# Linear attention and Mish layers on Trainium2: separate kinds of PSUM banks for a block's two output tiles, and an earlier start for the dense stage's first rows

## The chip, the cores and the metric

The kernel runs on one core of one Trainium2 chip. The metric is device time in microseconds (us) of one execution; the median of several runs is compared. A profiled execution gives the trace that the text quotes: start and end of the instructions on each engine and of the transfers.

## The reference, cut to what matters

`x` has 2048 rows of 640 numbers (float32). Two layers are run, each with the same weights: a Hedgehog linear attention with 32 heads of 20, then a dense part with 1536 hidden units.

```python
def _A_ref(x, wqkv, w_phi, wo):                      # on the layernorm of x
    q, k, v = split_heads(x @ wqkv)                  # 32 heads of 20
    pq, pk = q @ w_phi, k @ w_phi                    # per head, 20 x 20
    phi_q = concatenate([softmax(pq), softmax(-pq)]) # 40 features per head
    phi_k = concatenate([softmax(pk), softmax(-pk)])
    kv, z = phi_k^T v, sum_s phi_k                   # over all 2048 rows
    o = (phi_q kv) / (phi_q z + 1e-6)
    return merge_heads(o) @ wo

def _B_ref(x, w1, b1, w2):                           # on the layernorm of x
    h = x @ w1 + b1                                  # 640 -> 1536
    return (h * tanh(softplus(h))) @ w2              # Mish, 1536 -> 640

x = x + _A_ref(layernorm(x), ...)
x = x + _B_ref(layernorm(x), ...)
x = x + _A_ref(layernorm(x), ...)
x = x + _B_ref(layernorm(x), ...)
```

## The kernel before

**Tiles.** The rows are taken in 8 blocks (`NB`) of 256 rows, each block as 2 tiles (`BT`) of 128. A product in float32 is made of three matmuls: each operand is held as a high part and a low part, and high times high, high times low and low times high are added in PSUM. So a weight is a pair of tiles (`r1h`/`r1l`, `r2h`/`r2l`), and transposed rows are a pair `xth`/`xtl`.

**Stages.** In each layer `attend_first` computes the features of queries and keys, adds up the sums over keys in PSUM, and stores each block's query features, transposed, to a DRAM tensor `e_d[b]`. The query tiles of the last block are finished late, by a generator `rest`, of which each `next(rest)` moves what is pending on by one step; its last steps issue the four stores (line 400) of a query tile. Then `attend_second` runs over the blocks, and `dense` follows, with hidden products (L631), Mish (L644 to L657) and the second product (L673), then a residual add.

**A block of `attend_second`.** The change lies here. For block b there are these pieces:

- `load(b)` (L431 and on) fetches the query features `e_d[b]` into two `big` tiles and an `ol` tile. `fetch` (L358) brings the block's 256 rows of x, 640 KB, into one of two x buffers (`xt`).
- `average(b, t)`: 44 matmuls (L531) give numerators and denominators of tile t in PSUM, in an `mm` tile; VectorE evacuates them (L540, L541, L544) into a row tile `xn`, of which there are four.
- `Transposed(...).all()`: three steps, each with TensorE transposes (L275) into a `one` tile, ScalarE's copy to the high part (L113, `xth`), and VectorE's subtraction for the low part (L281, `xtl`). These have an order of their own on ScalarE (`act`).
- `project_half` (L318): 15 matmuls for one half (320 columns) of the output of one tile, with the weights `o_ws`.
- the residual: VectorE adds the PSUM result to the x rows. For tile 0 both halves lie in one `mm` tile and are added at once, 640 wide (L587), with statistics after it (L248, L250). For tile 1 each half lies in a `one` tile and is added by itself (`add_half`, L552, with its statistics in L553; L600 joins them). GpSimd and VectorE make the layernorm's scale and offset (`norm_scale`, L257 to L260). The rows are stored to `x1_d` (L602), from which the dense part reads them.
- `makes[b]` and `fetches[b + 1]`: the dense part's weights, fetched raw (L138) and split by ScalarE (L113) and GpSimd (L146), one of eight groups per block.

Averages run one block ahead: in block b's turn TensorE makes `average(b + 1, ...)`, products of block b, and the transposes of block b + 1 between the two halves of tile 1.

**PSUM** has eight banks: two `mm` tiles of two banks each, and four `one` tiles of one bank each. A new tile waits until the readers of the tile that had its buffer are done.

**What sets the order.** Inside `attend_second` the instructions of TensorE (PE) and of the DMA queue of SyncE (SP) stand in the order in which the code issues them (`manual_schedule`). VectorE (DVE), ScalarE (ACT) and GpSimd (POOL) are ordered by a planner, which simulates the program in time, except for the chain of `act`. Each engine works through its own instructions in order: one that waits holds up those behind it.

**The passage to `dense`.** After block 6's turn the kernel calls `begin_next`, which fetches the first block of the stored rows `x1_d` into a `big` tile and normalizes its two tiles on ScalarE into two row tiles (`xn`). The object it returns is used in block 7's turn: `nxt.all()` transposes it, ahead of block 7's products, so that `dense` can begin right behind them.

```python
                if b < NB - 1:
                    cur = nxt
                if b == NB - 2:
                    nxt = begin_next()
```

Of the kernel before, what the change touches and what calls it, by code (L numbers as in the profile page):

```python
# [8 lines left out]
F32 = mybir.dt.float32  # L9
F32R = mybir.dt.float32r  # L10
AF = mybir.ActivationFunctionType
ALU = mybir.AluOpType
# [4 lines left out]
P = 128  # L17
# [25 lines left out]
def kernel(  # L43
# [22 lines left out]
    def mm_tile():  # L66
        return psum.tile([P, 2, 512], F32, tag="mm", name="mm", bufs=2)

    def one_tile():
        return psum.tile([P, 512], F32, tag="one", name="one", bufs=4)  # L70
# [173 lines left out]
    def norm_stats(t, xt):  # L244

        bn = work.tile([P, 2, 6], F32, tag="bn", name="bn", bufs=2)
        for c in range(2):
            nc.vector.bn_stats(bn[:, c], xt[:, t, c * HC:(c + 1) * HC])  # L248
        mv = work.tile([P, 2], F32, tag="mv", name="mv", bufs=3)
        nc.vector.bn_aggr(mv, bn)  # L250
        return mv
# [60 lines left out]
    def project_half(ps, xts, t, ws, col, c, ks=range(KD)):  # L312
        sl = slice(t * P, (t + 1) * P)
        cs = slice(col + c * HC, col + (c + 1) * HC)
        for k in ks:
            h, l, wh, wl = xts.hs[k], xts.ls[k], ws[k][0][:, cs], ws[k][1][:, cs]
            for n, (a, r) in enumerate(((h, wh), (h, wl), (l, wh))):
                nc.tensor.matmul(ps[:, :HC], a[:, sl], r, start=(k == 0 and n == 0),  # L318
                                 stop=(k == KD - 1 and n == 2))
# [194 lines left out]
                nc.vector.tensor_copy(kvb[:80, 5, :42], ps[:80, 1, :42])  # L514
        yield

    def attend_second(x_src, x_dst, acc, fetches, makes, begin_next):
        kva, kvz, o_ws, loaded, rest = acc
        rows = {}

        def average(b, t):

            phs = loaded[b]
            po = mm_tile()
            for g in range(G):
                n = 120 if g < 10 else 80
                w = GW if g < 10 else 42
                c, j = divmod(g, 8)
                for q in range(2):
                    s0 = t * P + 64 * q  # L530
                    nc.tensor.matmul(  # L531
                        po[64 * q:64 * q + 64, c, GW * j:GW * j + w], phs[g][:n, s0:s0 + 64],
                        kvb[:n, g // 2, 64 * (g % 2):64 * (g % 2) + w], start=True, stop=True)
            o = row_tile()
            den = work.tile([P, H], F32, tag="r", name="den", bufs=2)
            pv = [po[:, c, :(DH + 1) * n].rearrange("p (h d) -> p h d", d=DH + 1)
                  for c, n in ((0, 24), (1, 8))]
            hh = (slice(0, 24), slice(24, H))
            for c in range(2):
                nc.vector.tensor_scalar_add(den[:, hh[c]], pv[c][:, :, DH], DEN_EPS)  # L540
            nc.vector.reciprocal(den, den)  # L541
            for c in range(2):
                n = hh[c].stop - hh[c].start
                nc.vector.tensor_tensor(o.rearrange("p (h d) -> p h d", d=DH)[:, hh[c]], pv[c][:, :, :DH],  # L544
                                        den[:, hh[c]].unsqueeze(2).to_broadcast([P, n, DH]), op=ALU.mult)
            rows.setdefault(b, []).append(o)
            if t == BT - 1:
                del loaded[b]

        def add_half(ps, xt, t, c, bn):  # L550
            cs = slice(c * HC, (c + 1) * HC)
            nc.vector.tensor_tensor(xt[:, t, cs], ps[:, :HC], xt[:, t, cs], op=ALU.add)  # L552
            nc.vector.bn_stats(bn[:, c], xt[:, t, cs])  # L553

        with tc.manual_schedule(engines={mybir.EngineType.PE, mybir.EngineType.SP}):
            kv = finish_kv(kva, kvz, mask)
            next(rest)
            next(kv)
            loaded[1] = load(1)
            xs = {0: fetch(x_src, 0)}  # L560
            fetches[0]()
            next(rest)
            next(kv)
            next(rest)
            average(0, 0)
            average(0, 1)
            loaded[2] = load(2)
            average(1, 0)
            cur = Transposed(rows.pop(0)).all()
            average(1, 1)  # L570
            loaded[3] = load(3)
            for b in range(NB):
                if b == NB - 1:
                    nxt.all()
                elif b:
                    average(b + 1, 0)
                xt = xs.pop(b)
                py = mm_tile()
                project_half(py[:, 0], cur, 0, o_ws, 0, 0)
                if 0 < b < NB - 1:  # L580
                    average(b + 1, 1)
                    if b + 3 < NB:
                        loaded[b + 3] = load(b + 3)
                if b + 1 < NB:
                    xs[b + 1] = fetch(x_src, b + 1)
                project_half(py[:, 1], cur, 0, o_ws, 0, 1)
                nc.vector.tensor_tensor(xt[:, 0, :].rearrange("p (c d) -> p c d", c=2), py[:, :, :HC],  # L587
                                        xt[:, 0, :].rearrange("p (c d) -> p c d", c=2), op=ALU.add)
                mvs = [norm_stats(0, xt)]
                bn = work.tile([P, 2, 6], F32, tag="bn", name="bn", bufs=2)  # L590
                pa = one_tile()
                project_half(pa, cur, 1, o_ws, 0, 0)
                add_half(pa, xt, 1, 0, bn)
                if b + 1 < NB:
                    nxt = Transposed(rows.pop(b + 1)).all()
                pa = one_tile()
                project_half(pa, cur, 1, o_ws, 0, 1)
                add_half(pa, xt, 1, 1, bn)
                mv = work.tile([P, 2], F32, tag="mv", name="mv", bufs=3)
                nc.vector.bn_aggr(mv, bn)  # L600
                norm_scale(b, mvs + [mv])
                nc.sync.dma_start(row_block(x_dst, b), xt)  # L602
                makes[b]()
                if b + 1 < NB:
                    fetches[b + 1]()
                next(rest, None)
                next(rest, None)
                if b < NB - 1:
                    cur = nxt
                if b == NB - 2:  # L610
                    nxt = begin_next()
            for _ in rest:
                pass
        return nxt


    def dense(x_src, x_dst, w1s, w2s, first, last):
# [117 lines left out]
    with tc.block(schedule_with_timeline_sim=True):  # L735
        src, first = x, None
        for layer in range(LAYERS):
            last = layer == LAYERS - 1
            dst = out if last else x2_d
            acc = attend_first(layer, src, first)  # L740
            if layer == 0:
                nc.sync.dma_start(b1s, b1)
            w1s = []
            w2s = {}

            steps = [("w1", (k,)) for k in range(KD)] + [("w2", fs) for fs in ((0, 1, 2), (3, 4), (5, 6))]

            spares = {("w1", n): [lambda t=t: r1_spare(f"r1{t}")] for n, t in enumerate(("l4", "h4", "l3", "l4"))}
            spares["w1", 4] = [lambda t=t: r2_spare(f"r2{t}") for t in ("h2", "l2", "h3")]
            spares.update({("w2", n): [s] for n, s in enumerate(five_spares(0))})  # L750
            spares["w2", 5] = [lambda: r2_wide(11, F32)[:, 0]]
            spares["w2", 6] = [row_tile]
            raws = {}

            def fetch_step(kind, ns):
                for n in ns:
                    rows = (w1 if kind == "w1" else w2)[n * P:(n + 1) * P, :]
                    raws[n] = fetch_rows(rows, [s() for s in spares[kind, n]])

            def make_step(kind, ns):  # L760
                for n in ns:
                    if kind == "w1":
                        w1s.append(r1_pair(n))
                    else:
                        w2s[n] = w2_pair(n)
                    make_parts((w1s if kind == "w1" else w2s)[n], raws.pop(n), True)

            x1t = []

            def begin_dense():  # L770
                x1t.append(fetch(x1_d, 0, big_tile().rearrange("p (t d) -> p t d", t=BT)))
                return normed(0, x1t[0])

            begun = attend_second(src, x1_d, acc, [lambda s=s: fetch_step(*s) for s in steps],
                                  [lambda s=s: make_step(*s) for s in steps], begin_dense)
            first = dense(x1_d, dst, w1s, w2s, [x1t[0], begun, None], last)
            src = dst

# [37 lines left out]
```

## Time and profile before

| | |
|---|---|
| three runs | 1473.74, 1473.95 (median), 1474.34 us |
| profiled execution | 1471.67 us, of which the span of the trace is 1469.6 us |
| granted TensorE clock, mean | 0.994 of full speed |
| instructions | 27963 |
| data moved | 135.26 MB, mean 92 GB/s |

The page gives busy time and its share of the span by engine. PE stands for TensorE's matmuls, PEld for its weight loads, which overlap them. A line of instructions has the form "line, engine, operation, output<-input"; "L318" is line 318 of the kernel. In the table of waits a row reads "who waits <- for whom: total us, number of times, longest". In the chain of waits a row is a start in us, a duration, and the work that the end of the program hung on at that time. In a table by windows a row has the window, its length, then the busy time and count of PE, PEld, DVE, ACT and POOL, the granted clock, the busy share of the 16 DMA engines and GB/s. In a timeline a row is a start, a duration, the engine, and in brackets the idle time before it and what ended it.

`attend_second` lies at about 270 to 398 us of the span in the first layer and at 990 to 1118 us in the second.

### The profile page before, as it was taken

The page shows a single profiled execution, that of the slowest core. Times are in us where ns is not written, and L with a number is a line of the kernel's source. Part 1 is how long each engine was busy: PE and PEld are TensorE (multiplying, and loading weights), DVE is VectorE, ACT ScalarE, POOL GpSimd, SP SyncE. Part 2 cuts the span into 40 slices and gives each one's busy share as a digit, 9 for nine tenths or more (in the row PEclk, how much of TensorE's full clock was granted, in tenths as well). Part 3 has the DMA queues.
Part 4 walks back from the last instruction along what each step waited for, and adds up shares of the span by engine and source line. Part 5 has one row for each costly group of instructions (what it writes and reads, how often), then busy time and mean ns, then how long its engine had stood idle before and what let it go on. Part 6 is the DMA issues. An engine that isn't in the chain of part 4 may idle for free.

```text
span 1469.6 us, 27963 instructions
## 1 busy us (share of the span) xinstructions
PE 1421.3 (97%) x11748; PEld 1394.3 (95%) x11748; DVE 1053.7 (72%) x1750; ACT 581.2 (40%) x973; POOL 455.1 (31%) x344
## 2 busy tenths in 40 slices
PE   7999999999799999999999999998988999999998
PEld 7999999889799999999999999998978999999998
DVE  4898877667487777777769777867665766666665
ACT  3534334212253444444454344332124444444443
POOL 1454433243242221222235334332443321111111
PEclk9999999999999999999999999999998999999999
DMA  9543334899410000011453342358973001011000
GB/s 297 164 89 57 54 51 71 196 247 249 157 35 19 37 37 10 28 37 37 156 195 66 57 70 54 55 100 203 264 230 118 8 13 37 37 37 37 37 14 24
DMA packets 215023, 135.26 MB, mean 92 GB/s; under 512 B 169977, under 2 KB 190969, under 8 KB 214897
## 3 DMA queue, kind: packets, MB, share of 16 engines
q1 hardware_dynamic: 214897, 133.47, 34.4%
q8 instruction: 92, 1.51, 0.4%
q14 instruction: 34, 0.28, 0.1%
HBM read 84.95 MB, written 48.50 MB: 91 GB/s over the span
## 4 chain that ended last, share of the span: by engine, by line
PE 79%; DVE 10%; ACT 4%; issue 3%; DMA 2%; POOL 1%; SPq 0%; DVEq 0%; POOLq 0%; ACTq 0%
PE mm L318 31%; PE mm L673 17%; PE one L631 17%; PE one L318 6%; PE one L275 3%; PE one L387 3%; PE mm L531 3%; DVE big L646 2%; DVE big L653 1%; DVE big L654 1%; ACT big L644 1%; DVE big L647 1%; DVE big L655 1%; ACT big L648 1%; DMA xt<-in_x 1%
## 5 line engine op out<-in xcount | busy, mean ns | idle before, releaser
L673 PE MATMUL mm<-r2h,ol 128*128 128x320 f32 x1280 | 302.9, 310 | 0.7 <-POOL ol L657 0.5
L657 POOL TENSOR_TENSOR ol<-big,ol 128x512 fp32r<-128x512 f32 (+1 forms) x98 | 127.4, 1300 | 493.5 <-ACT ol L656 393.4
L631 PE MATMUL one<-xtl,r1h 128*128 128x256 f32 x960 | 268.8, 280 | 1.9 <-DVE xtl L281 1.8
L631 PE MATMUL one<-xth,r1h 128*128 128x256 f32 x960 | 270.1, 281 | 0.1
L631 PE MATMUL one<-xth,r1l 128*128 128x256 f32 x960 | 268.3, 279 | 0.0
L673 PEld LDWEIGHTS mm<-r2h,ol 128*128 128x128 f32 x1280 | 219.1, 188 | 1.9 <-POOL ol L657 1.6
L673 PE MATMUL mm<-r2l,ol 128*128 128x320 f32 x640 | 197.9, 309 | 0.0
L318 PE MATMUL mm<-r1h,xth 128*128 128x320 f32 x600 | 189.1, 315 | 0.0
L318 PE MATMUL mm<-r1h,xtl 128*128 128x320 f32 x600 | 186.0, 310 | 0.0
L318 PE MATMUL mm<-r1l,xth 128*128 128x320 f32 x600 | 185.8, 310 | 0.0
L631 PEld LDWEIGHTS one<-xtl,r1h 128*128 128x128 f32 x960 | 180.7, 188 | 2.7 <-DVE xtl L281 2.7
L631 PEld LDWEIGHTS one<-xth,r1h 128*128 128x128 f32 x960 | 180.7, 188 | 0.7 <-ACT xth L113 0.5
L631 PEld LDWEIGHTS one<-xth,r1l 128*128 128x128 f32 x960 | 180.7, 188 | 0.0
L646 DVE TENSOR_SCALAR big<-big 128x512 f32<-128x512 f32 (+1 forms) x98 | 82.1, 837 | 132.7 <-ACT big L644 124.0
L318 PE MATMUL mm<-r2h,xth 128*128 128x320 f32 x460 | 147.2, 320 | 0.0
L318 PE MATMUL mm<-r2l,xth 128*128 128x320 f32 x460 | 142.9, 311 | 0.0
L318 PE MATMUL mm<-r2h,xtl 128*128 128x320 f32 x460 | 142.8, 310 | 0.0
L648 ACT ACTIVATE big<-big,two 128x512 f32<-128x512 f32 (+1 forms) x98 | 70.1, 716 | 164.3 <-DVE big L647 164.2
L113 ACT ACTIVATE xth<-one 128x512 fp32r<-128x512 f32 x144 | 70.3, 522 | 162.8 <-PE one L275 162.4
L656 ACT ACTIVATE ol<-big 128x512 fp32r<-128x512 f32 (+1 forms) x98 | 61.0, 622 | 173.1 <-DVE big L655 172.9
L353 POOL TENSOR_TENSOR r<-r,r 128x1280 f32<-128x1280 f32 x32 | 76.5, 2391 | 161.1 <-DVE r L352 160.9
L673 PEld LDWEIGHTS mm<-r2l,ol 128*128 128x128 f32 x640 | 120.4, 188 | 0.0
(122 smaller groups left out, 3097.1 us busy)
## 6 DMA issues: line engine op xcount, KB each, us to landing
e_d<-r SPq DMA_DIRECT2D x128, 160.0 KB, 4.0
big<-e_d SPq DMA_DIRECT2D x32, 600.0 KB, 8.7
xt<-x_d SPq DMA_DIRECT2D x30, 640.0 KB, 3.9
x_d<-xt SPq DMA_DIRECT2D x23, 640.0 KB, 3.8
xt<-in_x SPq DMA_DIRECT2D x16, 640.0 KB, 4.4
raw<-in_w SPq DMA_DIRECT2D x20, 320.0 KB, 8.3
raw<-in_w SPq DMA_DIRECT2D x8, 768.0 KB, 9.8
out<-xt SPq DMA_DIRECT2D x6, 640.0 KB, 2.9
```

The source lines that it names most:

```text
L113: ins = nc.scalar.activation(*args, **kw)
L275: nc.tensor.transpose(ps[:, c, t * P:(t + 1) * P], self.rows[t][:, (c0 + c) * P:(c0 + c + 1) * P], ident)
L318: nc.tensor.matmul(ps[:, :HC], a[:, sl], r, start=(k == 0 and n == 0), stop=(k == KD - 1 and n == 2))
L353: nc.gpsimd.tensor_tensor(eg, eg, r.unsqueeze(2).to_broadcast([P, 2 * H, DH]), op=ALU.mult)
L387: nc.tensor.matmul(acc[64 * n:64 * n + m, c:c + w], v[:, GW * g:GW * g + m], e[:, 120 * g:120 * g + w], start=(i == 0 and p in (0, 4)), st ...
L531: nc.tensor.matmul(po[64 * q:64 * q + 64, c, GW * j:GW * j + w], phs[g][:n, s0:s0 + 64], kvb[:n, g // 2, 64 * (g % 2):64 * (g % 2) + w], s ...
L631: nc.tensor.matmul(ph[:, j, :], l, r, start=(n == 0), stop=(n == 3 * KD - 1))
L646: nc.vector.tensor_scalar_min(e, e, E_CAP)
L648: nc.scalar.activation(r, n, AF.Ln, bias=two)
L656: nc.scalar.activation(ah[:, js], n, AF.Copy)
L657: nc.gpsimd.tensor_tensor(al[:, js], n, ah[:, js].bitcast(F32), op=ALU.subtract)
L673: nc.tensor.matmul(pys[t][:, c, :HC], l[:, j, sl], r, start=(f == 0 and n == 0), stop=(f == KF - 1 and n == 2))
```

## The change

Four things differ, all in and around `attend_second`.

1. Tile 0's two halves go to two `one` tiles, each with its own 320-wide add and statistics; tile 1's two halves go to the two banks of one `mm` tile, also with an add for each half. A small class `Rows` holds the buffers of a tile's statistics and issues the product and the add.
2. The fetch of the dense part's first rows is a function of its own, called in block 5's turn behind the fetch of block 6's x rows.
3. The normalization of these rows is called in block 6's turn, behind tile 0's second half. It has its own name (`ahead`), and block 7 transposes it as before.
4. In block 0's turn `next(rest)` is called once instead of twice. So the steps of `rest` come one call later from there on, and the stores of a query tile move from block 0's turn to block 1's.

```diff
-        def add_half(ps, xt, t, c, bn):
-            cs = slice(c * HC, (c + 1) * HC)
-            nc.vector.tensor_tensor(xt[:, t, cs], ps[:, :HC], xt[:, t, cs], op=ALU.add)
-            nc.vector.bn_stats(bn[:, c], xt[:, t, cs])
+        class Rows:
+            def __init__(self, b, t):
+                self.t, self.xt, self.ps = t, xs[b], None
+                self.bn = work.tile([P, 2, 6], F32, tag="bn", name="bn", bufs=2)
+
+            def half(self, c, ps):
+                project_half(ps, cur, self.t, o_ws, 0, c)
+                part = self.xt[:, self.t, c * HC:(c + 1) * HC]
+                nc.vector.tensor_tensor(part, ps[:, :HC], part, op=ALU.add)
+                nc.vector.bn_stats(self.bn[:, c], part)
+
+            def mean(self):
+                mv = work.tile([P, 2], F32, tag="mv", name="mv", bufs=3)
+                nc.vector.bn_aggr(mv, self.bn)
+                return mv
...
             for b in range(NB):
                 if b == NB - 1:
-                    nxt.all()
+                    ahead.all()
                 elif b:
                     average(b + 1, 0)
-                xt = xs.pop(b)
-                py = mm_tile()
-                project_half(py[:, 0], cur, 0, o_ws, 0, 0)
+                r0, r1 = Rows(b, 0), Rows(b, 1)
+                r0.half(0, one_tile())
                 if 0 < b < NB - 1:
                     average(b + 1, 1)
                     if b + 3 < NB:
                         loaded[b + 3] = load(b + 3)
                 if b + 1 < NB:
                     xs[b + 1] = fetch(x_src, b + 1)
-                project_half(py[:, 1], cur, 0, o_ws, 0, 1)
-                nc.vector.tensor_tensor(xt[:, 0, :].rearrange("p (c d) -> p c d", c=2), py[:, :, :HC],
-                                        xt[:, 0, :].rearrange("p (c d) -> p c d", c=2), op=ALU.add)
-                mvs = [norm_stats(0, xt)]
-                bn = work.tile([P, 2, 6], F32, tag="bn", name="bn", bufs=2)
-                pa = one_tile()
-                project_half(pa, cur, 1, o_ws, 0, 0)
-                add_half(pa, xt, 1, 0, bn)
+                if b == NB - 3:
+                    fetch_next()
+                r0.half(1, one_tile())
+                mv0 = r0.mean()
+                if b == NB - 2:
+                    ahead = begin_next()
+                py = mm_tile()
+                r1.half(0, py[:, 0])
                 if b + 1 < NB:
                     nxt = Transposed(rows.pop(b + 1)).all()
-                pa = one_tile()
-                project_half(pa, cur, 1, o_ws, 0, 1)
-                add_half(pa, xt, 1, 1, bn)
-                mv = work.tile([P, 2], F32, tag="mv", name="mv", bufs=3)
-                nc.vector.bn_aggr(mv, bn)
-                norm_scale(b, mvs + [mv])
+                r1.half(1, py[:, 1])
+                norm_scale(b, [mv0, r1.mean()])
+                xt = xs.pop(b)
                 nc.sync.dma_start(row_block(x_dst, b), xt)
                 makes[b]()
                 if b + 1 < NB:
                     fetches[b + 1]()
-                next(rest, None)
-                next(rest, None)
+                for _ in range(2 if b else 1):
+                    next(rest, None)
                 if b < NB - 1:
                     cur = nxt
-                if b == NB - 2:
-                    nxt = begin_next()
             for _ in rest:
                 pass
-        return nxt
+        return ahead
...
+            def fetch_dense():
+                x1t.append(fetch(x1_d, 0, big_tile().rearrange("p (t d) -> p t d", t=BT)))
+
             def begin_dense():
-                x1t.append(fetch(x1_d, 0, big_tile().rearrange("p (t d) -> p t d", t=BT)))
                 return normed(0, x1t[0])
```

More of the change, by code (lines that the diff above doesn't have):

```diff
@@ L515, in finish_kv, with attend_second @@
         yield
-    def attend_second(x_src, x_dst, acc, fetches, makes, begin_next):
+    def attend_second(x_src, x_dst, acc, fetches, makes, fetch_next, begin_next):
         kva, kvz, o_ws, loaded, rest = acc
@@ L768 @@
             x1t = []
+            def fetch_dense():
+                x1t.append(fetch(x1_d, 0, big_tile().rearrange("p (t d) -> p t d", t=BT)))
             def begin_dense():
-                x1t.append(fetch(x1_d, 0, big_tile().rearrange("p (t d) -> p t d", t=BT)))
                 return normed(0, x1t[0])
             begun = attend_second(src, x1_d, acc, [lambda s=s: fetch_step(*s) for s in steps],
-                                  [lambda s=s: make_step(*s) for s in steps], begin_dense)
+                                  [lambda s=s: make_step(*s) for s in steps], fetch_dense, begin_dense)
             first = dense(x1_d, dst, w1s, w2s, [x1t[0], begun, None], last)
```

## The prediction

> **What bounds the kernel now.** The page comes first: TensorE is busy for 97% of the span.
>
> ```profile
> PE 1421.3 (97%) x11748; PEld 1394.3 (95%) x11748; DVE 1053.7 (72%) x1750; ACT 581.2 (40%) x973; POOL 455.1 (31%) x344
> ```
>
> So only PE's 48 us without work, and matmuls that run slowly, can be won. The waits of PE, asked for in the two windows that hold `attend_second` (255 to 405 us for the first layer, 970 to 1120 us for the second), say where most of it lies. Columns: total us, times, longest.
>
> ```profile
> PE one L275 <- ACT xn L113: 8.7, 2, 8.4
> PE mm L531 <- DVE xn L544: 3.4, 2, 2.7
> PE one L275 <- DVE xt L552: 0.9, 1, 0.9
> ```
>
> ```profile
> PE one L275 <- ACT xn L113: 8.7, 2, 8.4
> PE one L318 <- DVE xt L552: 2.2, 2, 1.7
> PE one L275 <- DVE xt L552: 1.3, 1, 1.3
> PE mm L531 <- DVE xn L544: 0.7, 1, 0.7
> ```
>
> The long wait is the same in both layers. The chain of waits (start, us, what) shows it around the change of block 6 to block 7:
>
> ```profile
> 364.68 1.41 PE mm L531 x44
> ...
> 374.50 1.09 PE one L275 x10
> 375.60 2.22 PE one L318 x15
> ...
> 380.15 4.97 DMA big<-x_d
> ...
> 385.21 1.74 ACT xn L113 x2
> 386.95 0.04 issue
> 387.00 2.18 PE one L275 x9
> 389.18 4.72 PE mm L318 x30
> ```
>
> ```profile
> 1094.96 2.22 PE one L318 x15
> ...
> 1106.39 2.18 PE one L275 x9
> 1108.57 5.09 PE mm L318 x30
> ```
>
> Block 6's last product ends at 377.82. SP then stores the block, issues weight loads, and only then the fetch of the dense block's rows (4.97 us); ACT normalizes them (1.74), PE transposes them. Block 7's first product starts at 389.18: 11.36 us after block 6's last. In the second layer it is 1097.18 to 1108.57, 11.39 us. Between 364.68 and 377.82, block 6 itself runs without a gap, 13.14 us.
>
> **Part 1, fetch and normalization brought forward.** In the changed program's order of instructions the dense rows' fetch stands on SP in block 5, right behind the x rows of block 6, and the two normalizations stand on ACT ahead of the copies of block 7's transposed rows. The store, the weight loads, the fetch and ACT's first half leave the path. What is late next: there are four row buffers; one holds a weight row and two the averaged rows of block 7, so the second normalization waits until PE has transposed those, and ACT's copies are queued behind it. The DVE and ACT rows of a block give the durations:
>
> ```profile
> 1052.27 1.36 ACT L113 ACTIVATE xth<-one 128x512 fp32r<-128x512 f32 x3 [8.92 <-PE one L275]
> ```
>
> ```profile
> 1052.90 1.62 DVE L281 TENSOR_TENSOR xtl<-one,xth 128x512 fp32r<-128x512 f32 x3
> 1055.13 0.49 DVE L552 TENSOR_TENSOR xt<-one,xt 128x320 f32<-128x320 f32 x1 [0.61 <-PE one L318]
> 1055.65 0.49 DVE L553 BATCH_NORM_STATS2 bn<-xt 128x6 f32<-128x320 f32 x1
> 1056.18 0.21 DVE L600 BATCH_NORM_AGGREGATE mv<-bn 128x2 f32<-128x12 f32 x1
> 1056.55 0.26 DVE L540 TENSOR_SCALAR den<-mm 128x24 f32<-128x24 f32 x2 [0.16 <-PE mm L531]
> 1056.84 0.35 DVE L541 RECIPROCAL den<-den 128x32 f32<-128x32 f32 x1
> 1057.23 0.89 DVE L544 TENSOR_TENSOR xn<-mm,den 128x480 f32<-128x480 f32 x2
> 1059.66 0.23 DVE L260 SCALAR_TENSOR_TENSOR stats<-mv,stats 128x1 f32<-128x1 f32 x2 [1.55 <-POOL stats L258]
> 1065.29 0.82 DVE L587 TENSOR_TENSOR xt<-mm,xt 128x640 f32<-128x640 f32 x1 [3.36 <-DMA xt<-x_d]
> ```
>
> Count from the start of block 7's transposes (374.50 in the first layer). They end at 1.1; the last product of block 6 runs from 1.1 to 3.3. ACT normalizes the second tile from 1.05 to 1.9 (half of 1.74) and copies until 3.3 (1.36). The first two DVE subtractions run 2.5 to 3.9 (two long ones of the 1.62), then block 6's last add (0.49), then the third to 4.8. The dense block's transposes (1.09) begin at 3.3 and end by 4.4, held a little by the buffers that the subtractions free. Block 7's first product follows the third subtraction, at 4.8, that is 1.5 us after block 6's last one instead of 11.4: 9.9 us per layer. The weight copies that ACT has between the two sets of rows are hidden by block 7's products, 2.2 us a half.
>
> Slow matmuls go too: the first 30 took 4.72 and 5.09 us against twice 2.2, so 0.3 + 0.7. Part 1 takes away 2 x 9.9 + 1.0 = **20.8 us**. Bounds: only the transposes' 1.09 left, 21.6; the buffer wait as long again, about 1.5 more in each layer, 17.8.
>
> **Part 2, banks.** The average's second tile now waits for the output tile of the block before, not for the evacuation of the first average. The 3.4 us in the first layer (POOL's work in DVE's queue held that evacuation) and the 0.7 in the second go. In block 0 the first tile's adds stand ahead of a stream transpose, so the 0.9 and 1.3 us of the transposes' waits go. First layer 4.3, second 2.0 at most.
>
> Splitting the 640-wide add costs 2 x 0.49 - 0.82 = 0.16 us of DVE per block, 2.6 us over 16. DVE is not what a block waits for:
>
> ```profile
> 351.60:364.70 13.10, 13.10 (x160) 12.61 (x162) 8.94 (x24) 2.90 (x7) 4.84 (x7) 1.00 0.80 260
> ```
>
> DVE (third busy column) works 8.94 of 13.10 us, so I take nothing. The Trainium skill speaks against such a split ("VectorE: DVE Perf Modes", "The TRN2 errata"): a fixed cost per instruction, so tiles should have at least 512 elements. The trace agrees on the cost, 0.16; by the rule as a price on the path the gain would be 2.6 us less.
>
> **Part 3, what the new order costs.** The first half's add needs the block's x rows, and now stands in DVE's queue *ahead of* the evacuation of the second average, for which the transposes wait. Before, the whole add came behind it. So late rows hurt sooner. And one `next(rest)` moves: the four stores of the last but one query tile go from block 0 to block 1, ahead of that block's loads on SP.
>
> ```profile
> DMA to landing us min/median/max: 4.1/4.7/6.4
> ```
>
> ```profile
> DMA to landing us min/median/max: 3.8/8.8/11.2
> ```
>
> ```profile
> 1028.00:1080.00 52.00, 49.58 (x609) 47.50 (x610) 34.07 (x91) 9.78 (x15) 20.70 (x18) 1.00 1.03 273
> ```
>
> ```profile
> 1017.25 7.36 SPq L400 DMA_DIRECT2D e_d<-r  x4
> ```
>
> ```profile
> 1079.18 0.82 DVE L587 TENSOR_TENSOR xt<-mm,xt 128x640 f32<-128x640 f32 x1 [2.19 <-issue]
> ```
>
> ```profile
> 1081.58 2.47 PE one L318 x15
> ```
>
> The row fetches land after 4.7 us in the first layer, 8.8 in the second, where the DMA engines are full from 1028 to 1080 (share 1.03). There the adds of blocks 4 and 5 (1065.29, 1079.18) already come late; the last half product of block 5 starts 2.4 us after its add began (1081.58). In the new order it must wait for add, statistics, scale terms, evacuation, add, statistics, mean and add: 0.49 + 0.49 + 0.23 + 1.50 + 0.49 + 0.49 + 0.21 + 0.49 = 4.4, with the gaps between them 4.7. If the landings stay where they are, block 5 ends 2.3 us later and the 2.0 of part 2 are swallowed, since the landings, not PE, set the pace. It is no sum over blocks: a PE that waited in block 4 is less early in block 5. If the landings move up with PE (the queue is emptier before block 2, without the four stores), the 2.0 stay. So the second layer lies between -2.0 and +2.3; I take +1.0, nearer the row of a full DMA. In the first layer PE would come to blocks 3 and 4 4.3 us earlier than now, and the rows (4.1 to 6.4) can give some of it back, 0 to 2.7; I take 1.0: -3.3. The extra fetch in block 5 falls behind the full stretch; nothing.
>
> **Sum:** -20.8 - 3.3 + 1.0 = -23.1 us, against the profiled execution's 1471.67 (span 1469.6): 1448.6. The runs' median is 2.28 above that execution, so 1473.95 - 23.1 = **1450.9**.
>
> **Rivals.** *Rows later still.* The four stores (7.36 us of issuing at 1017.25) stand ahead of block 2's loads and push the rows of blocks 3 to 5 back by, say, 4.5 us in both layers, an estimate from half to all of that row. Second layer: 2.3 + 4.5 = 6.8 lost; first: 4.3 gained, some 5.6 lost. -20.8 + 1.3 + 6.8 = -12.7: 1461. For it: the share of 1.03. Against: the same bytes move in the same order but for these four, and the queue had slack just before. Chance 0.13.
>
> *Slower: the loop of two x buffers.* A block's rows can be fetched only when the store of two blocks before has landed. Store (about 10 us in the second layer, taken like a fetch) and fetch (up to 11.2) make 21.2; the new order allows about 2.3 less than the old before PE stops. If this loop, not the DMA's total, sets the landings, each of blocks 1 to 6 loses 2.4 us in both layers: 12 x 2.4 = 29 lost, 20.8 gained, 1482. It decides against the change from 1.8 us a block. For it: waits of 1.7 and 0.5 in the second layer now. Against: the first layer's rows have none, with 4.7. Chance 0.05.
>
> *The fetch doesn't come early.* If the dense rows' buffer or queue still held them until block 6's store, the long wait would stay and parts 2 and 3 give -2.3: 1471.6. Against: the fetch's buffer was last read in block 4. Chance 0.04.
>
> **The numbers.** The forecast has 0.78. Its own range comes from the bounds: 21.6 + 4.3 + 2.0 + the 2.2 us of late adds = -30 (1444) to -17.8 - 1.6 + 2.3 = -17 (1457). To leave out no more than 2 in 10 it reaches to the first rival: 1444 to 1461. About 0.2%, 2.9 us, is what a measurement tells from no change. Faster: 0.78 + 0.13 = 0.91; same 0.04; slower 0.05.
>
> **What would show it.** In the profile after: no wait of some 8 us of L275 for xn; block 7's first product 1 to 3 us after block 6's last; the first 30 matmuls of block 7 in 4.4 us; no 2.7 us wait of L531. Part 3 shows as DVE's first-half add waiting for a DMA with the transposes late, in the second layer's blocks 3 to 5. I am wrong if a wait of over 4 us stands in place of the old one, or if blocks 3 to 6 take clearly over 13.1 us in the first layer.

## The result, and the profile after

| | time, us | ratio to before, 95% interval |
|---|---|---|
| before | 1474.14 (median) | |
| changed | 1453.07 (1452.21 to 1454.22) | 0.9854 (0.9837 to 0.9871) |

The changed kernel is 21.1 us faster by the medians. Its profiled execution took 1452.65 us, with a span of 1450.8, 18.8 less than the span before. The two gains differ by 2.3 us, mostly because the profiled execution of the kernel before (1471.67 us, clock 0.994) is faster than all its other runs (1473.74 to 1479.73 us; the clocks on record are 0.988 to 0.993). The time of the kernel before drifted by a few us between sets of runs, which were taken on different chips (medians 1474.1 to 1476.8), so kernels are compared below by their ratio to it in the same set.

The page of the changed kernel gives TensorE the same work in the shorter span:

```profile
PE 1419.8 (98%) x11748; PEld 1393.1 (96%) x11748; DVE 1052.7 (73%) x1766; ACT 580.4 (40%) x973; POOL 455.4 (31%) x344
```

The waits of PE over `attend_second`, first layer and then second layer (who <- for whom: total us, times, longest):

```profile
PE one L275 <- DVE xn L544: 2.3, 1, 2.3
PE one L275 <- DVE xtl L281: 2.3, 2, 1.2
PE mm L318 <- DVE xt L560: 1.0, 2, 0.6
```

```profile
PE one L275 <- DVE xn L544: 3.4, 2, 2.4
PE one L275 <- DVE xtl L281: 2.2, 2, 1.2
PE mm L318 <- DVE xt L560: 0.9, 2, 0.6
```

The 8.4 us wait of the transposes for ACT's normalized rows is gone in both layers, and so are the waits of L531. New ones stand there: the transposes wait for `xn`, the averaged rows that VectorE evacuates, and products wait for the residual add (L560). They lie in blocks 3 and 4. The chain of waits shows block 4 of the first layer:

```profile
334.81 9.50 DMA xt<-in_x
...
344.44 0.50 DVE xt L560
...
346.17 0.89 DVE xn L544 x2
...
348.63 3.81 PE mm L318 x15
```

The fetch of the block's x rows took 9.50 us. The first half's add (344.44) waited for it, the evacuation behind it in VectorE's queue (346.17) waited for the add, and the transposes for the evacuation. VectorE's timeline has the same adds with the idle time before them, for block 3 and block 4, and the view of the row fetches (L358) the time from issue to landing, for those whose landing it can tell:

```profile
327.95 0.49 DVE L560 TENSOR_TENSOR xt<-one,xt 128x320 f32<-128x320 f32 x1 [4.08 <-DMA xt<-in_x]
...
344.44 0.49 DVE L560 TENSOR_TENSOR xt<-one,xt 128x320 f32<-128x320 f32 x1 [6.78 <-DMA xt<-in_x]
```

```profile
DMA to landing us min/median/max: 3.9/4.2/10.6
```

The 10.6 us belong to the rows of block 2. Before, no work waited for x rows in the first layer. The same view has 6.4 us at most there, but it leaves out the rows of blocks 1 to 5; when these landed is told below, with part 3.

The wait costs more than its own length. PE's two gaps in block 4 are 2.32 and 0.55 us, but the block takes 4.70 us more than 13.12: the 15 matmuls behind the gaps took 3.81 us, against 2.48 for the same product one block earlier, at a granted clock of 0.56 and then 0.66 (the column behind the five engines):

```profile
348.00:350.00 2.00, 1.45 (x6) 1.37 (x6) 1.95 (x5) 2.00 (x6) 0.66 (x2) 0.56 1.11 207
350.00:352.40 2.40, 2.40 (x14) 2.21 (x12) 0.63 (x2) 0.38 (x2) 2.40 (x2) 0.66 1.10 220
```

To follow where time was won and given back, take the start of each block: the first matmul of the first average made in its turn (L531), counted from the very first average of the layer. Two rows of PE's timeline give one such number; these are the first average and block 5, in the first layer, before and then after (the counts at the end are cut by the window asked for):

```profile
274.10 0.28 PE L531 MATMUL mm<-kvb,big 120*64 120x63 f32 x2
...
351.49 0.39 PE L531 MATMUL mm<-kvb,big 120*64 120x63 f32 x6
```

```profile
274.45 0.33 PE L531 MATMUL mm<-kvb,big 120*64 120x63 f32 x4
...
352.38 0.44 PE L531 MATMUL mm<-kvb,big 120*64 120x63 f32 x7
```

351.49 - 274.10 = 77.39 before, 352.38 - 274.45 = 77.93 after. All starts, in us, read in the same way; "b7" is block 7's first product, "end" the start of `dense` (in the changed order 25 of its matmuls come ahead of the last product; they are set against it):

| start of | block 1 | 2 | 3 | 4 | 5 | 6 | b7 | end |
|---|---|---|---|---|---|---|---|---|
| first layer, before | 21.35 | 37.21 | 51.15 | 64.27 | 77.39 | 90.51 | 114.73 | 124.03 |
| first layer, after | 20.05 | 33.17 | 46.29 | 60.11 | 77.93 | 91.05 | 105.56 | 114.44 |
| second layer, before | 21.75 | 34.87 | 48.86 | 61.98 | 77.05 | 90.93 | 115.18 | 124.86 |
| second layer, after | 20.05 | 33.17 | 46.29 | 61.40 | 79.12 | 92.24 | 106.76 | 115.64 |

The ends differ by 9.59 and 9.22 us, 18.81 together: all of the 18.8 by which the span is shorter. Up to block 3 the changed kernel is 4.86 and 2.57 us ahead. Blocks 3 and 4 give all of this back, and 0.54 and 1.31 more. What is left, 9.59 and 9.22 us, comes out of the 10.13 and 10.53 us won between block 6's start and the end.

### The profile page after: what moved, and what is told of

Same layout as the page of the kernel before. It is cut to its first block, busy times and chain, and to the rows that moved or that the text cites. A ratio compares the mean times of both kernels' runs of the same rounds, so it can differ in the third digit from the quotient of the medians.

```text
span 1450.8 us, 27982 instructions
## 1 busy us (share of the span) xinstructions
PE 1419.8 (98%) x11748; PEld 1393.1 (96%) x11748; DVE 1052.7 (73%) x1766; ACT 580.4 (40%) x973; POOL 455.4 (31%) x344
## 4 chain that ended last, share of the span: by engine, by line
PE 79%; DVE 11%; DMA 4%; ACT 3%; issue 2%; POOL 0%; DVEq 0%; SPq 0%; ACTq 0%; POOLq 0%
PE mm L318 31%; PE mm L680 17%; PE one L638 17%; PE one L318 6%; PE one L387 3%; PE one L275 2%; PE mm L531 2%; DMA xt<-in_x 2%; DVE big L653 2%; DMA xt<-x_d 1%; DVE big L660 1%; DVE big L661 1%; ACT big L651 1%; DVE big L654 1%; DVE big L662 1%
```

## The experiments

Three theories for the lost time of blocks 3 and 4 are named in the expectations. T1: the x rows are late, since the DMA engines are full and the rows stand behind other traffic. T2: the four stores that moved by a block hold them up. T3: the rows are no later, but the first half's add now asks for them sooner. The theories do not exclude each other. In the table at the end "load first" and "rows first" name the order of x rows and load on SP, and "banks" stands for points 1 and 4 of the change together.

**The early fetch and normalization alone.** The kernel before, with

```diff
                     xs[b + 1] = fetch(x_src, b + 1)
+                if b == NB - 3:
+                    fetch_next()
                 project_half(py[:, 1], cur, 0, o_ws, 0, 1)
...
                 mvs = [norm_stats(0, xt)]
+                if b == NB - 2:
+                    ahead = begin_next()
...
-                if b == NB - 2:
-                    nxt = begin_next()
```

> The kernel before, with the dense block's fetch in block 5 and its normalization in block 6, and nothing else of the change. By the forecast's part 1: 20.8 us less, 1453.3, the 8.4 us wait of the transposes gone in both layers. If the two traces are read rightly (9.7 us and 0.4 to 0.8 of slow matmuls per layer), 20.6 less and so the same time as the whole change, within 1.5 us. Rival, that the banks have to be separated for the early normalization to bring anything: less than 15 us of it.

Measured: 1454.19 us, ratio 0.9859 (0.9842 to 0.9875), the same as the whole change, and 0.0141 x 1474 = 20.8 us less than before. In its trace the way from block 6's start to the end is 10.30 and 10.72 us shorter, 21.0 together. PE's waits in the first layer have the early ones of the kernel before, and not the long one:

```profile
PE mm L531 <- DVE xn L544: 3.4, 2, 2.7
...
PE one L275 <- DVE xt L552: 0.9, 1, 0.9
```

So the early fetch carries the gain by itself, without new banks.

**The banks alone.** The changed kernel with the early fetch taken out again:

```diff
-                if b == NB - 3:
-                    fetch_next()
...
-                if b == NB - 2:
-                    ahead = begin_next()
...
+                if b == NB - 2:
+                    fetch_next()
+                    ahead = begin_next()
```

> The changed kernel with the dense block's fetch and normalization back behind block 6: only the banks, the split add and the moved step of the query work. The forecast's parts 2 and 3 gave -3.3 and +1.0 us, so 2.3 less than before, 1471.8. The two traces, read block by block, give +0.5 in the first layer and +1.3 in the second, so some 1.9 us more than before, 1476.0. Told apart by the sign against before.

Measured: 1476.93 us, ratio 1.0005 (0.9993 to 1.0016): no gain. 0.9984, which the forecast's 2.3 us would be, lies outside; the 1476.0 us read from the two traces fit. Blocks 1 to 3 begin at 20.05, 33.16 and 46.28 us, without the early stalls, and block 5 at 77.96, as late as with the old banks.

**The late query work as before.**

```diff
-                for _ in range(2 if b else 1):
+                for _ in range(2):
                     next(rest, None)
```

> The changed kernel, with the late query work advanced twice in block 0 again, so that the two groups of four stores lie some 30 us apart on SP (blocks 0 and 2) as before the change, not 13 us (blocks 1 and 2). Theory T1 (the x rows of blocks 3 and 4 land when the DMA engines, full from block 1 on, have worked off all that stands ahead of them, in whatever order): no change within 1.5 us, 1451.5 to 1454.5, the rows of block 4 in the first layer land again some 70 us after the first average, and the waits of the transposes for xn stay (2.3 us in the first layer, 3.4 in the second). Theory T2 (the moved stores hold them up): these waits go, some 5 us come back in the first layer and 2 to 4 in the second: 1444 to 1447.

Measured: 1453.25 us, ratio 0.9843 (0.983 to 0.9856): no change. In the first layer the stall moves to block 2 (block 3 begins at 50.11 instead of 46.29), and block 5 begins at 78.35. T2 falls: the moved step isn't what costs the time.

**The first half's add behind the second average's evacuation.**

```diff
-                r0.half(0, one_tile())
+                pa = one_tile()
+                project_half(pa, cur, 0, o_ws, 0, 0)
...
-                    average(b + 1, 1)
+                    with tc.issue_after(average(b + 1, 1)):
+                        r0.add(0, pa)
```

> The changed kernel with the first half's add of tile 0 put behind the evacuation of the second average in VectorE's order, in blocks 1 to 6. Theory T3 (the rows are no later than they were, but asked for sooner, and the wait for them holds the evacuation that the transposes need): the waits of the transposes for xn (2.3 us and 3.4 us) go, and 4 to 6 us come back in all: 1447 to 1449. Theory T1 or T2 alone (rows so late that block 4 would wait for them anyway, now with a PSUM buffer of the transposes): 0 to 3 us come back, 1450 to 1453, and the waits carry another name.

Measured: 1453.65 us, ratio 0.9847 (0.9834 to 0.986): no change in the time. The waits for `xn` did go; these stand in the first layer now:

```profile
PE mm L318 <- DVE xt L564: 1.6, 1, 1.6
PE one L275 <- DVE xt L564: 1.1, 1, 1.1
```

(L564 is the add in this kernel.) Block 5 begins at 75.68 and 78.18 instead of 77.93 and 79.12: 2.25 and 0.94 us, of which 0.34 is left at the second layer's end; the times don't show the 2.6 us that the two ends are earlier. By the trace the place of the add is a part of the cause, the smaller one; with late rows the transposes next wait for the PSUM buffer that the add has to free.

**Less traffic ahead of the rows.** The second group of four stores is put off to the end of block 4, with its load behind it; in a second kernel to the end of block 3, with the load left in block 4.

```diff
-                    if b + 3 < NB:
+                    if b + 3 < NB - 1:
                         loaded[b + 3] = load(b + 3)
...
-                for _ in range(2 if b else 1):
+                for _ in range((1, 2, 1, 0, 1, 1, 1, 1)[b]):
                     next(rest, None)
+                if b == NB - 4:
+                    loaded[NB - 1] = load(NB - 1)
```

> The changed kernel, with the second group of four stores put off from the end of block 2 to the end of block 4, and the load that reads them behind it there. Theory T1 (the rows of block 4 land when the DMA engines have worked off what stands ahead): that traffic no longer stands ahead of them, so block 5 begins 3 to 5 us earlier in the first layer (it began 77.9 us after the first average; without any wait it would be 72.5) and 2 to 3 us in the second: 1445 to 1448, unless block 6's averages now wait for the late load, up to 5 us in each layer, which would give it all back (1455). Rival, that the rows wait for their buffer (the store of two blocks before) and not for traffic: block 5 begins when it did, 1452 to 1455.

> The same, but the second group of four stores only goes to the end of block 3, behind the rows of block 4 and ahead of those of block 5, and its load stays in block 4. Theory T1: block 5 begins 3 to 5 and 2 to 3 us earlier, and the rows of block 5 lose up to 2 us of it again where the DMA engines are still full: 1446 to 1450. Rival of the buffers: no change within 1.5 us.

Measured: 1463.39 us, ratio 0.9911 (0.9894 to 0.9927), and 1454.84 us, 0.9858 (0.9844 to 0.9873). Block 5 begins at 74.44 and 74.54 in the one kernel, at 74.57 and 73.86 in the other: 3.4 to 5.3 us earlier than in the changed kernel, as T1 has it (in the second layer more than it had), and the rival of the buffers falls. But both times lie above what was expected, since what was put off is late in its turn. In the first kernel block 6's average waits for its load, in PE's timeline:

```profile
366.60 0.59 PE L531 MATMUL mm<-kvb,big 120*64 120x63 f32 x6 [4.64 <-DMA big<-e_d]
```

and block 6 begins at 92.27 and 92.47; in the second block 5's rows are late, 92.89 and 91.87.

**More traffic.**

```diff
+                    if b in (1, 2):
+                        nc.sync.dma_start(row_block(spare_d, b), row_block(x_src, b))
                     if b + 3 < NB:
                         loaded[b + 3] = load(b + 3)
```

> The changed kernel, with traffic added that nobody waits for: in blocks 1 and 2 of each layer a copy of a block's 640 KB of rows from DRAM to DRAM, ahead of the block's load. Theory T1: the rows of blocks 3 and 4 land later by the time that these copies take of the DMA engines, an estimate of 1.7 to 3.5 us each from the rows' own fetches; block 5 begins 3 to 7 us later in each layer: 1459 to 1467. Rival, that buffers or the order on VectorE set the pace and the engines have room: 1452 to 1455.

Measured: 1457.54 us, ratio 0.9875 (0.986 to 0.989), 3 to 4.5 us slower than the changed kernel (by the ratios and by the medians), less than T1 expected and more than its rival. The first layer is as expected: block 5 begins at 82.27, 4.3 us later, with the transposes waiting longer for `xn` (L276 and L545 are L275 and L544 here):

```profile
PE one L276 <- DVE xn L545: 6.4, 2, 4.0
```

In the second layer block 4 begins 2.9 us later (64.25), and block 5 at 78.54, 0.6 us earlier than without the copies. Total traffic is no full account of the second layer.

**The rows first.** In blocks 1 to 4 the next block's x rows are fetched ahead of the load, which is needed two blocks later:

```diff
                     average(b + 1, 1)
-                    if b + 3 < NB:
-                        loaded[b + 3] = load(b + 3)
                 if b + 1 < NB:
                     xs[b + 1] = fetch(x_src, b + 1)
+                if 0 < b < NB - 3:
+                    loaded[b + 3] = load(b + 3)
```

> The changed kernel with one order turned round on SP: in blocks 1 to 4 the fetch of the next block's x rows stands ahead of the load of the query features that are needed two blocks later. Theory T1 in the form that the runs so far leave (the rows land late because they stand in a full queue behind a load that nobody needs yet): the rows of blocks 3 and 4 land some 5 us earlier in the stretch, the waits for xn and xt in blocks 3 and 4 go, and block 5 begins 72.5 us after the first average in the first layer and at 73 to 75 in the second, against 77.9 and 79.1: 5 and 4 to 6 us less, 1442 to 1446, if the loads, now later, still land in time. Rival (the total traffic up to block 5 binds, whatever its order): what the rows gain the loads lose, an average waits for its load in block 4 or 5 instead, and the time stays at 1451 to 1455. Rival (a row fetch waits for its buffer, and now holds the load behind it): 1455 to 1460.

Measured: 1444.86 us, ratio 0.9784 (0.977 to 0.9799), against 0.9854 (0.9837 to 0.9871) for the changed kernel: faster than both kernels. SP's queue (DMA-issuing rows) around the rows of block 4 in the first layer, the changed kernel and then this one:

```profile
323.17 9.45 SPq L400 DMA_DIRECT2D e_d<-r  x4
332.72 1.47 SPq L491 DMA_DIRECT2D big<-e_d  x2
334.25 0.47 SPq L493 DMA_DIRECT2D ol<-e_d  x1
334.81 0.66 SPq L358 DMA_DIRECT2D xt<-in_x  x1
```

```profile
324.05 10.50 SPq L400 DMA_DIRECT2D e_d<-r  x4
334.67 0.59 SPq L358 DMA_DIRECT2D xt<-in_x  x1
335.36 1.29 SPq L491 DMA_DIRECT2D big<-e_d  x2
```

The rows are issued 59.31 us after the first average instead of 60.36, and the load now stands behind them. Block 4's rows land after 7.4 us instead of 9.50, those of block 2 after 7.7 instead of 10.6 (first line: landing of the first layer's fetches as far as the view can tell it, second line: of block 4's; then PE's waits there, and the first average and block 5 in PE's timeline):

```profile
DMA to landing us min/median/max: 4.3/5.6/7.7
DMA to landing us min/median/max: 7.4/7.4/7.4
```

```profile
PE one L275 <- DVE xtl L281: 2.2, 2, 1.2
PE mm L318 <- DVE xt L560: 0.8, 2, 0.6
```

```profile
275.36 0.33 PE L531 MATMUL mm<-kvb,big 120*64 120x63 f32 x4
...
348.76 0.45 PE L531 MATMUL mm<-kvb,big 120*64 120x63 f32 x8
```

Block 5 begins at 73.40 (73.13 in the second layer), 4.5 and 6.0 us earlier than in the changed kernel, and the loads, now behind, hold nobody up. Not all is gone: block 4 still takes 14.00 us in the first layer, since its rows land after the first half's product has ended.

**The rows first, with parts of the change.** The same order with the early fetch alone, with the add put behind, with nothing else, and with the banks alone:

> The kernel before with the early fetch and normalization alone (old banks), and the same order turned round on SP. If the banks' gain is real and was only swallowed by late rows, this kernel keeps the early stalls of the old banks (some 5 us in the first layer, 2 to 3 in the second, 6 to 8 together) and stays that much behind the changed kernel with the rows first. If the banks bring nothing of their own, the two are within 1.5 us. By itself I expect 1450 to 1453.

> The changed kernel with the rows first on SP, and the first half's add of tile 0 behind the second average's evacuation on VectorE. If the rows are now in time, the place of the add doesn't matter: the same as the rows first alone within 1 us. If rows still come late in the second layer, up to 2 us less than that.

> The kernel before with the rows ahead of the load on SP in blocks 1 to 4, and nothing else. Its rows were late only in the second layer's blocks 4 and 5 (waits of 1.7 and 0.5 us), so by the theory of the queue's order 0 to 2 us less than before: a ratio of 0.9985 to 1.000. Rival (the turned order is a gain by itself, whatever the banks): 4 us or more less, a ratio under 0.997.

> The changed kernel without the early fetch and normalization, with the rows ahead of the load: the banks alone, but with their rows in time. If late rows are what swallowed the banks' gain, 6 to 8 us less than before, a ratio of 0.9945 to 0.996, where the banks alone made no difference. If the banks gain only together with the early fetch: a ratio of 0.998 to 1.000.

Measured: with the early fetch alone 1450.61 us, 5.8 behind the rows first in the changed kernel; with the add behind 1445.41 us, ratio 0.9784 (0.9767 to 0.98), the same as without; alone 1475.16; with the banks alone 1465.42, a little less than was expected. The ratios side by side:

| | load first | rows first |
|---|---|---|
| nothing else | 1 | 0.9993 (0.9984 to 1.0001) |
| banks | 1.0005 (0.9993 to 1.0016) | 0.9934 (0.992 to 0.9947) |
| early fetch | 0.9859 (0.9842 to 0.9875) | 0.9829 (0.9813 to 0.9844) |
| banks and early fetch | 0.9854 (0.9837 to 0.9871) | 0.9784 (0.977 to 0.9799) |

With the load first, the banks bring nothing, with or without the early fetch. With the rows first they bring 0.9993 - 0.9934 = 0.0059, 8.7 us, and 0.9829 - 0.9784 = 0.0045, 6.6 us. The turned order is worth nothing on the old kernel; with the early fetch alone the two intervals touch, and what it brings there is not settled. With the banks alone and the rows first, block 5 begins at 72.57 and 72.52, which is four blocks of 13.12 us behind block 1's 20.05: in these blocks nothing waits any more.

## Why the prediction was right, and the step that was not

**Part 1** was right in mechanism and size. From block 6's start to block 7's first product it was 90.51 to 114.73, 24.22 us, and is 91.05 to 105.56, 14.51: 9.71 us less; 9.73 in the second layer; the forecast had 9.9. The chain after shows the path that was named as next:

```profile
375.39 1.00 PE one L275 x9
376.39 0.03 issue
376.41 0.13 ACT xn L113
...
377.24 0.58 ACT xth L113
...
378.46 0.68 DVE xtl L281
379.14 0.40 DVE xt L560
379.54 0.34 DVE xtl L281
379.88 0.14 issue
380.01 4.64 PE one L318 x30
```

PE transposes block 7's rows, ACT's second normalization has waited for that, its copies follow, VectorE's subtractions with the last add between them, and block 7's product. In PE's timeline the transposes begin at 375.23, and the product stands 4.78 us behind; the count in the forecast said 4.8. The slow matmuls were right too: the first 30 of block 7 took 4.48 us instead of 4.90 and 5.28, 1.2 where 1.0 was expected. Part 1 is 9.71 + 9.73 + 1.22 = 20.7, forecast 20.8, and the kernel with this part alone gives 20.8 by its runs.

**Part 2**, the early stalls, went as forecast, a little above its bounds: by block 3's start 4.86 and 2.57 us (4.3 and 2.0 at most). The split add's 0.16 us per block are not on the path: a block without waits takes 13.12 us before (64.27 to 77.39) and after (33.17 to 46.29). So the rule that the Trainium skill gives in "VectorE: DVE Perf Modes" ("The TRN2 errata") against small tiles was no price here, since VectorE has room.

**Part 3 is the term that was mis-sized**, in the first layer, and the step that failed is a reading. The mechanism was named, a first-half add that asks for the rows sooner, ahead of the evacuation for which the transposes wait. But the forecast took 4.1/4.7/6.4 us as the landing of the rows in the first layer, and allowed 0 to 2.7 us, 1.0 taken. 5.40 us were lost there (4.86 ahead, then 0.54 behind). The forecast's own sign of being wrong came: block 4 took 17.82 us.

The row 4.1/4.7/6.4 holds four fetches, the rows of blocks 0, 6 and 7 and the dense part's. For others the view finds no landing. Asked for 300 to 350 us of the kernel before, it lists the fetches of blocks 2 to 5 and no line of landings behind them:

```profile
L358 SPq DMA_DIRECT2D xt<-in_x x4: 356/476/522, 306.1 to 347.4; - x4
```

The trace also records each signal of a finished part of a transfer. Taken from these, issue and landing in the first layer, in us after the first average (the one for block 4 in the changed kernel is the 9.50 of the chain above):

| issue + landing | rows of block 3 | block 4 | block 5 |
|---|---|---|---|
| before | 43.67 + 9.59 = 53.26 | 62.00 + 8.71 = 70.71 | 73.34 + 10.87 = 84.21 |
| changed | 43.80 + 9.59 = 53.39 | 60.36 + 9.50 = 69.86 | 71.49 + 11.09 = 82.58 |
| changed, rows first | 42.05 + 5.54 = 47.59 | 59.31 + 7.41 = 66.72 | 73.29 + 5.24 = 78.53 |

So these rows took 8.7 to 10.9 us before the change too, as in the second layer, and the DMA engines were as full as there (last column but one), which the forecast had not asked for:

```profile
330.00:340.00 10.00, 10.00 (x120) 9.71 (x117) 7.44 (x21) 2.73 (x4) 1.76 (x2) 1.00 1.00 203
340.00:350.00 10.00, 10.00 (x105) 9.75 (x105) 6.66 (x20) 1.26 (x4) 3.00 (x4) 1.00 1.05 300
```

In the second layer, where the row 3.8/8.8/11.2 does hold them, the net was a loss of 1.31, forecast 1.0. These are the fetch of block 4's rows on SP and their add on VectorE, before:

```profile
336.10 0.52 SPq L358 DMA_DIRECT2D xt<-in_x  x1
```

```profile
346.10 0.82 DVE L587 TENSOR_TENSOR xt<-mm,xt 128x640 f32<-128x640 f32 x1 [0.82 <-PE mm L318]
```

The old add ran 346.10 - 338.37 = 7.7 us after the block's start, and waited for PE, not for rows; but the rows had landed only 1.3 us before it (70.71 against 72.00). The new first-half add can run when its product ends, 3.9 us after the start. With PE 4.2 us earlier by then, the rows are asked for some 8 us sooner. SP issues them only 1.6 us sooner: 334.81 - 274.45 = 60.36 us after the first average, against 336.10 - 274.10 = 62.00, in both behind stores and a load. They land 0.85 us sooner than before, at 69.86, where the add could run at 64.0. So the rows are no later than they were, as T3 says, but they do not move up with PE. The parts measured sum to -20.7 + 0.54 + 1.31 = -18.8, where -23.1 was forecast; the 4.3 between them is part 3 in the first layer (5.4 against 1.0) with small change elsewhere.

The median came nearer to the forecast than this sum, 1453.07 against 1450.9, and that is luck: the forecast counted from the median before, which lies 2.28 us above the profiled execution; after the change the two are 0.42 apart.

**The rivals.** "Rows later still" did not come true: it had the rows of blocks 3 to 5 pushed back by 4.5 us by the four moved stores, but counted from the first average the rows land 0.13 us later to 1.63 us sooner than before in the first layer, and 0.87 to 1.68 us sooner in the second, and the kernel with these stores in their old place is as slow. That its 4.3 won and 5.6 lost in the first layer are near the 4.86 and 5.40 measured is a coincidence. The loop of two x buffers did not decide: putting off other traffic moved block 5 by 3.4 to 5.3 us with the buffers as they were. The fetch did come early.

**The order on SP** is what holds the rows back, as far as the runs show. The Trainium skill states in "DMA: Bandwidth & Descriptors" ("Queues, rings and completion order") that each DMA engine takes the descriptors of a queue in ring order. The runs agree: by the table above, rows put ahead of the load land 3.1 to 5.8 us sooner, of which 2.1 to 5.9 us are a shorter way from issue to landing, and at most 1.75 an earlier issue.

What stays open: how much of what is left is due to the time that SP spends on issuing the stores ahead of the rows. An issue of the stores from another engine's queue, which would tell, was not tried. Nor do the runs explain why added copies cost the second layer nothing.

## What to carry to other kernels

Before a forecast rests on a row of landing times, see which transfers the row holds: here it left out those that mattered, and the share of the DMA engines in the same stretch, 1.00 and 1.05, would have been a warning. A change that makes the consumer earlier, or moves a transfer's first reader up in an engine's queue, uses up slack that no wait shows: block 4's rows had 1.3 us of it before. So for each stall that is removed, follow the transfers of the next blocks back to the queue that issues them, and see what stands ahead there that is needed later. A part that measures as nothing may be worth its whole forecast once the transfer behind it is put in the right order: the banks went from no gain to 6.6 and 8.7 us by exchanging two statements.

## What the runs showed of the hardware that was not expected

The time that SP takes to issue the same four stores (160 KB each, in pieces of 128 bytes) differs with what was issued ahead of them. The second group of the first layer took 6.80 us before, 9.45 in the changed kernel (its row stands above), 13.86 with the added copies ahead, and 4.79 when it was put off to block 4. That the backlog of the queue sets this time is a reading of these four numbers, not shown by itself. SP's rows before, and with the copies:

```profile
327.04 6.80 SPq L400 DMA_DIRECT2D e_d<-r  x4
```

```profile
322.39 13.86 SPq L401 DMA_DIRECT2D e_d<-r  x4
```

Everything behind them on SP waits that long, so a store whose data are needed much later can hold up a fetch that is needed in the next block.
